# Half-height weight loads and wider zero products at the start of a fused attention and feed-forward kernel

## The chip, the cores and the metric

The kernel runs on one core of a Trainium2 chip. A core has a matrix engine (TensorE, PE in the profile; its weight loads stand apart as PEld), three engines for everything else (VectorE or DVE, ScalarE or ACT, GpSimd or POOL), a sequencer that issues most transfers (SyncE, SP), and 16 DMA engines that carry them. The metric is the device time of one execution in microseconds (us), the median of several runs.

## The reference

Eight batches with eight heads of attention over 576 positions, 64 channels each, then a two-layer feed-forward network over all 4608 tokens:

```python
scores = scale * np.matmul(q, k.transpose(0, 1, 3, 2))
rel = pos[:, None] - pos[None, :]
mask_local = (rel >= 0) & (rel < stride)              # heads 0 to 3, stride 32
mask_strided = (rel >= 0) & (pos[None, :] % stride == pos[:, None] % stride)   # heads 4 to 7
attn = softmax(where(mask, scores, -1e9)); attn_out = attn @ v
x = attn_out as 4608 x 512
h = x @ w_in                                          # 512 x 2048
g = where(h >= 1, h, where(h <= -1, 0, (h + 1) ** 2 / 4))
out = g @ w_out                                       # 2048 x 512
```

All inputs are 32-bit floats, but the feed-forward weights come as 64-bit ones and reach the kernel as pairs of 32-bit words.

## The kernel before, in words

The feed-forward work is cut along the 2048 inner columns into 16 units f of 128, and along the tokens into chunks of 512. A unit has two parts i: part 0 holds its columns of w_in, part 1 its rows of w_out, each as 128 partitions of 512 pairs of words, 4096 bytes a partition, 512 KB. `load_w(f, i)` (lines 312 to 320) brings one part into a tile named raw with one transfer on SP's queue. Its optional argument `after` first copies one element of a loaded q/k tile into the raw tile (line 318, on ACT), which holds the transfer, and all that stands behind it on SP, until that q/k tile has landed.

A raw part is then converted by steps named by letters: A (line 343, ACT) and L (line 347, ACT) scale the high and the low words, B (line 351, DVE) shifts, C (line 355, POOL) adds, D (line 364, ACT, or DVE under the name G) rounds to the matrix engine's 32-bit format, E (line 368, DVE) takes what the rounding left. "A10" is step A of unit 1, part 0. Every step reads all 128 partitions of its part. The products use high and low halves, three products for one.

The first three chunks of tokens are done unit by unit: `up` (line 775) makes h for a unit from x, ACT and DVE apply g, `down` (line 820) adds into four accumulators. Later chunks use weights combined beforehand (lines 388 to 408) in seven products in place of eight, lines 917 and 1005.

Attention runs batch by batch, in four units of rows u. Its steps are named by letters too: s scores (line 482), o and i open and close their accumulators with products of zeros and of the mask (lines 497 and 506), g copies out (line 538), x, a or b, e, q, p or k, r or w the softmax (lines 568 to 596), f flips by the matrix engine (line 609), c or d keeps the result (line 619), v multiplies by v (line 669), h and l write x as high and low parts (lines 730 and 739). From batch 1 on the probabilities are turned through DRAM: line 643 writes them, and line 654 gathers them with four transfers of 32 partitions each, to partitions 0, 32, 64 and 96 in this order.

The order of the work is written out by hand, and each engine does its instructions in that order. `BEGIN` (lines 29 to 34) is the order of the start, the attention of batch 0 with the conversions of units 0 to 2. In it "Zs0:17" is 17 products of zeros into the accumulators of score unit 0 (`zero`, lines 460 to 467), "Zv0" and "Zf0" the same into those of v and of the flips; the real work overwrites what they write. Later lists (`WORK`, `CONV`, `SUMS` and so on) hold times by which the rest is sorted once, when the program is built.

The loads of the start are issued on SP in this order (lines 1044 to 1059): q/k of batch 0 in four transfers; part 0 of unit 0, held by line 318; two transfers of v; part 0 of unit 1; two of v; part 0 of unit 2; then, in `stage`, part 1 of units 0, 1 and 2, both parts of unit 3; two q/k transfers of batch 1; both parts of units 4 and 5; then v of batch 1, and further units as their places come free.

Of the kernel before, what the change touches and what calls it, by code (L numbers as in the profile page):

```python
# [17 lines left out]
P = 128  # L18
# [8 lines left out]
GATE, ROUNDED = (0.31, 2.01), (1.62, 3.18)  # L27

BEGIN = """
Zs0:17 o0 s0 o1 i0 X0 s1 i1 S0 o3 g1 x1 s2 Zv0:3 Zf0:3 m2 e0 a1 A00 s3 i3 e1 x2 q0 p0 g3 a2 q1 Zf0:9  # L30
e2 w0 Zf0:5 f0 p1 x3 c0 B00 v0 b3 L00 e3 r1 q2 p2 f1 C00 r2 q3 A10 d1 D00 p3 h0 r3 L10 l0 A20 v1 B10
f2 h1 d2 f3 c3 v3 l1 H1 L20 C10 G10 v2 E10 M0 M1 h3 B20 l3 E00 h2 H3 C20 U0 l2 G20 V0 M3 U1 H2 M2
E20 V1
"""
# [139 lines left out]
def tile_sparse_attention_then_ffn(  # L174
# [14 lines left out]
    nc = tc.nc  # L189
# [28 lines left out]
    def slots(u):  # L218

        n, rest = divmod(UNITS[u][2], IL if UNITS[u][0] else IS)  # L220
        return n + (rest > 0), n
# [50 lines left out]
    for i in range(IL):  # L272
        part = slice(i * QL, (i + 1) * QL)
        for n0, n1, off in ((0, SLOTS, ST),) if i else ((0, 1, 0), (1, SLOTS, ST)):
            t = m_loc[part, n0:n1]
# [4 lines left out]
    for i in range(IS):  # L280
        t = m_str[i * QS:(i + 1) * QS]
# [20 lines left out]
    wt, raws, pieces, held = {}, {}, {}, set()  # L302
    PLACES = (6, 7, 8, 9, 10, 11, 12, 13, 14, 15, 12, 13, 14, 15)
    w_v = w.bitcast(U32).rearrange("f p (i e t) -> f p i e t", i=2, t=2)
# [4 lines left out]
    def place(u, shape, dtype, name):  # L309
        return slot(f"w{u}", shape, dtype, name)  # L310

    def load_w(f, i, after=None):
        at = PLACES[f]
        if i == 0:
            held.add(at)
            raws[f] = place(at, [P, 2, DM, 2], U32, f"raw_{f}")
        if after is not None:
            nc.scalar.copy(raws[f][0:1, i, 0:1, 0].bitcast(F32), after)
        nc.sync.dma_start(raws[f][:, i], w_v[f][:, i])
        pieces[f, i] = [(raws[f][:, i], slice(0, DM))]  # L320

    def load_piece(f, i, k=0, pool=qk_p, tag="qk", of=1):
# [51 lines left out]
    def stage(n=len(PLACES)):  # L374
        nonlocal staged
        while staged < n and ((staged, 0) in pieces or PLACES[staged] not in held):
            if (staged, 0) not in pieces:
                load_w(staged, 0)
            load_w(staged, 1)
            staged += 1  # L380
# [65 lines left out]
    def attention(b, kinds):  # L446
# [3 lines left out]
        def banks(u, kind):  # L450

            if (u, kind) in ahead:
                return ahead.pop((u, kind))
            local, _, nb = UNITS[u]
            Q, W = (QL, WL) if local else (QS, WS)
            shapes = {"s": [[P, slots(u)[0], 2, W]] * 2, "f": [[P, n, P] for n in slots(u)], "v": [[P, nb, Q]] * 2}[kind]
            name = {"s": "sc", "f": "tp", "v": "xp"}[kind]
            return [psum(kinds(u, kind, j), shape, f"{name}_{b}_{u}_{j}") for j, shape in enumerate(shapes)]

        def zero(u, kind, n):  # L460

            ahead[u, kind] = ts = banks(u, kind)
            names = [f"a{k}" for k in range(len(ts[0].shape) - 1)]
            t = ts[0].rearrange(f"p {' '.join(names)} -> p ({' '.join(names)})")
            N = min(t.shape[1], 256)
            for _ in range(n):
                nc.tensor.matmul(t[:, :N], zeros, zeros[:, :1].broadcast_to([P, N]), start=True, stop=True)

# [39 lines left out]
        def homes(u):  # L508
# [3 lines left out]
            ns = slots(u)  # L512
            N = 2 * sum(ns)
            size = [P, 2 * SLOTS * 2, 64]
            if b == 0 and u >= 2:
                room = place(NF - 1 - u, size, F32, f"pr_{b}_{u}")
            else:
                room = s_p.tile(size, F32, tag="s", name=f"pr_{b}_{u}")
            st = st_p.tile([P, 3, 2 * SLOTS * 2], F32, tag="st", bufs=4, name=f"st_{b}_{u}")[:, :, :N]
            pr = room[:, :N, :W]  # L520
            if W < 64:
                nc.gpsimd.memset(room[:, :N, W:], 0.0)
            todo = [(j, slice(0, P), 0, ns[1], j * ns[0]) for j in range(2)]
# [226 lines left out]
        def go(names):  # L750
            for name in names.split():
                if name[0] == "Z":
                    zero(int(name[2]), name[1], int(name[4:]))
                    continue
                steps[name[0]](int(name[1]))
# [287 lines left out]
    with tc.manual_schedule():  # L1043
        for p in range(4):
            load_qk(0, p)
        load_w(0, 0, loaded[0, 1, "qk"][0:1, 0, 0:1])
        load_v(0, 0)
        load_v(0, 1)
# [44 lines left out]
        for c in range(CLASSIC):  # L1093
            for f in range(NF):
                t = 4 * (NF * (c - 1) + f)
# [17 lines left out]
        for s in range(NSC):  # L1113
            t = 4 * NF * (CLASSIC - 1) + 2 * len(UP) * s
# [61 lines left out]
```

## Time and profile before

| | |
|---|---|
| median of 3 runs | 818.4 us (817.62 to 819.12) |
| span of the profiled execution, first to last instruction | 815.5 us, 2.9 less than the median |
| granted TensorE clock, mean | 1.000 |
| busy share of the span | PE 99%, PEld 81%, DVE 70%, ACT 61%, POOL 29% |
| HBM read and written | 147.26 MB and 46.66 MB, 238 GB/s over the span |
| first product of line 775 | starts at 24.06 us |

The profile is that of one execution. A row of a group gives the line, the engine, the operation, the tiles (out<-in, buffer numbers left out), shapes and count, busy time and mean duration, and the idle time of the engine before it with what ended it. A row of the timeline gives start, length, engine, line, and in square brackets the idle time before it with its releaser. SPq is SP's queue: its rows are issues of transfers, and the length is that of the issue, not of the transfer. A row on issues ends with the KB of one and the median time from issue to landing.

### The profile page before, as it was taken

What the parts mean: (1) busy time and instruction counts of PE and PEld (TensorE: products, weight loads), DVE (VectorE), ACT (ScalarE), POOL (GpSimd) and SP (SyncE); (2) the same over time, 40 slices, a digit from 0 to 9 for tenths busy, and PEclk for the clock granted to TensorE, in tenths of its full rate; (3) what the DMA queues carried; (4) which work ended last, traced back from release to release, by engine and by line L of the source; (5) the groups of instructions that cost most, each with busy time, mean ns of one, the idle gap of its engine ahead of it and who ended that gap; (6) DMA issues with size and microseconds to landing.
All of it is one profiled execution on the core that took longest, in us unless ns stands there. A gap on an engine that the chain in (4) does not pass through costs nothing.

```text
span 815.5 us, 17861 instructions
## 1 busy us (share of the span) xinstructions
PE 806.2 (99%) x6969; PEld 656.9 (81%) x6969; DVE 574.7 (70%) x850; ACT 495.4 (61%) x866; POOL 232.5 (29%) x226
## 2 busy tenths in 40 slices
PE   8999999999999999999999999999999999999998
PEld 6788888878878888887878888888888888888886
DVE  5898868767548477776778876675589834558664
ACT  5888955545355365776775453778654647775442
POOL 5353544873347543023222000220120001114100
PEclk9999999999999999999999999999999999999999
DMA  9936437788868867987998768887666776666765
GB/s 344 408 138 201 153 111 274 265 298 278 265 221 299 286 243 257 304 287 247 285 288 266 216 203 249 263 265 228 193 193 213 232 235 196 196 192 190 216 200 170
DMA packets 101796, 195.10 MB, mean 239 GB/s; under 512 B 17105, under 2 KB 32465, under 8 KB 99665
## 3 DMA queue, kind: packets, MB, share of 16 engines
q1 hardware_dynamic: 92496, 164.60, 63.3%
q10 hardware_dynamic: 9216, 29.36, 9.4%
q8 instruction: 55, 0.90, 0.5%
q14 instruction: 29, 0.23, 0.1%
HBM read 147.26 MB, written 46.66 MB: 238 GB/s over the span
## 4 chain that ended last, share of the span: by engine, by line
PE 91%; DMA 5%; issue 1%; DVE 1%; ACT 1%; POOL 0%; SPq 0%; ACTq 0%; POOLq 0%
PE o L820 16%; PE h L775 16%; PE yo L1005 15%; PE y L917 15%; PE zo L1005 8%; PE z L917 7%; PE xo L1005 4%; PE x L917 4%; PE xp L669 3%; PE sc L482 3%; DMA wr<-kq 1%; DMA qk<-in_qk_s 1%; DMA there<-t 1%; DMA pT<-there 1%; DMA qk<-in_qk_l 1%
## 5 line engine op out<-in xcount | busy, mean ns | idle before, releaser
L917 PE MATMUL y<-x,wr 128*128 128x512 f32 x576 | 141.3, 392 | 0.0
L775 PE MATMUL h<-xq,w 128*128 128x512 f32 x576 | 140.0, 392 | 0.1
L1005 PE MATMUL yo<-hl,wr 128*128 128x512 f32 x576 | 132.8, 390 | 0.6 <-DMA wr<-kq 0.6
L820 PE MATMUL o<-gh,w 128*128 128x512 f32 x384 | 130.1, 399 | 0.0
L1005 PEld LDWEIGHTS yo<-hl,wr 128*128 128x128 f32 x576 | 108.0, 188 | 23.4 <-DMA wr<-kq 1.0
L775 PEld LDWEIGHTS h<-xq,w 128*128 128x128 f32 x576 | 107.4, 188 | 23.4 <-DVE xq L739 0.7
L917 PEld LDWEIGHTS y<-x,wr 128*128 128x128 f32 x576 | 107.4, 188 | 22.7
L820 PEld LDWEIGHTS o<-gh,w 128*128 128x128 f32 x384 | 72.1, 188 | 16.2
L820 PE MATMUL o<-gl,w 128*128 128x512 f32 x192 | 75.0, 391 | 0.0
L917 PE MATMUL z<-x,wr 128*128 128x512 f32 x288 | 73.7, 391 | 0.0
L957 POOL TENSOR_TENSOR ga<-gb,ga 128x1024 f32<-128x1024 f32 x9 | 21.6, 2397 | 167.5 <-DVE ga L785 141.7
L1005 PE MATMUL zo<-hl,wr 128*128 128x512 f32 x288 | 66.1, 390 | 0.0
L572 POOL TENSOR_TENSOR pr<-pr,st 128x384 f32<-128x384 f32 (+3 forms) x21 | 26.3, 1253 | 135.7 <-DVE st L595 64.5
L1005 PEld LDWEIGHTS zo<-hl,wr 128*128 128x128 f32 x288 | 54.0, 188 | 11.3
L917 PEld LDWEIGHTS z<-x,wr 128*128 128x128 f32 x288 | 53.8, 188 | 11.3
L782 ACT ACTIVATE tmp<-tmp 128x512 f32<-128x512 f32 x96 | 60.7, 632 | 3.0
L871 DVE TENSOR_TENSOR hl<-ga,hl 128x1024 fp32r<-128x1024 f32 x36 | 47.3, 1315 | 19.9 <-ACT hl L870 18.2
L870 ACT CAST hl<-ga 128x1024 fp32r<-128x1024 f32 x36 | 38.0, 1056 | 35.1 <-PE yo L1005 12.6
L396 POOL TENSOR_TENSOR xs<-w 128x512 f32<-128x512 f32 x32 | 45.1, 1426 | 48.4 <-DMA ks<-xs 32.8
L785 DVE SCALAR_TENSOR_TENSOR h<-h,u 128x512 f32<-128x512 f32 x47 | 32.8, 697 | 30.5 <-ACT u L782 30.1
L398 POOL TENSOR_TENSOR xs<-xs 128x256 f32<-128x256 f32 x64 | 51.3, 802 | 5.0
L779 ACT ACTIVATE u<-h,half 128x512 f32<-128x512 f32 x48 | 33.1, 689 | 29.6 <-PE h L775 24.1
(120 smaller groups left out, 1321.9 us busy)
## 6 DMA issues: line engine op xcount, KB each, us to landing
wr<-ks SPq DMA_DIRECT2D x192, 256.0 KB, 3.9
wr<-kq SPq DMA_DIRECT2D x144, 256.0 KB, 3.4
ks<-xs ACTq DMA_DIRECT2D x16, 1024.0 KB, 4.8
raw<-in_w SPq DMA_DIRECT2D x30, 512.0 KB, 9.6
kq<-w ACTq DMA_DIRECT2D x48, 256.0 KB, 3.8
qk<-in_qk_s SPq DMA_DIRECT2D x16, 604.0 KB, 6.1
qk<-in_qk_l SPq DMA_DIRECT2D x16, 576.0 KB, 6.0
v<-in_v_l SPq DMA_DIRECT2D x21, 384.0 KB, 6.0
```

The source lines that it names most:

```text
L396: nc.gpsimd.tensor_tensor(out=b[:, :, f] if i else b[:, f], in0=hi, in1=lo, op=ALU.add)
L398: nc.gpsimd.tensor_tensor(out=st[:, to, HF:], in0=st[:, x, HF:], in1=st[:, y, HF:], op=op)
L572: eng.tensor_tensor(out=pr, in0=pr, in1=st[:, 0].unsqueeze(2).broadcast_to(list(pr.shape)), op=ALU.add)
L775: nc.tensor.matmul(o_ps[c, f], wt[f][:, 0, h, x, e:e + P], xq[c][:, y, cc], start=first and n == 0, stop=last and n == len(todo) - 1)
L779: nc.scalar.activation(u, h, AF.Relu, bias=half, scale=0.5)
L782: nc.scalar.activation(u, u, AF.Square)
L785: nc.vector.scalar_tensor_tensor(out=to, in0=h, scalar=1.0, in1=u, op0=ALU.max, op1=ALU.min)
L820: nc.tensor.matmul(o_ps[c][d], wt[f][:, 1, h, x, e:e + P], gs[y], start=f == 0 and n == 0, stop=f == NF - 1 and n == 2)
L870: nc.scalar.copy(t[:, 0], src)
L871: nc.vector.tensor_tensor(out=t[:, 1], in0=src, in1=t[:, 0].bitcast(F32), op=ALU.subtract)
L917: nc.tensor.matmul(to, w_[:, a, c * P:(c + 1) * P], xc[m][:, b, c], start=m in (1, 2, 5) and c + q == 0, stop=c == 1 and q == 2, skip_grou ...
L1005: nc.tensor.matmul(to, w_[jj][:, a, d * P:(d + 1) * P], t[:, b, jj], start=m in (1, 2, 5) and k + jj + q == 0, stop=k == NP // 2 - 1 and j ...
```

## The change

Loads of units 0 to 5 become two transfers each, of partitions 0 to 63 and 64 to 127. The products of zeros get up to 384 columns in place of 256 (every accumulator concerned has 384), and their counts in `BEGIN` go from 17, 3, 3, 9 and 5 to 11, 2, 2, 6 and 3.

```diff
 BEGIN = """
-Zs0:17 o0 s0 o1 i0 X0 s1 i1 S0 o3 g1 x1 s2 Zv0:3 Zf0:3 m2 e0 a1 A00 s3 i3 e1 x2 q0 p0 g3 a2 q1 Zf0:9
-e2 w0 Zf0:5 f0 p1 x3 c0 B00 v0 b3 L00 e3 r1 q2 p2 f1 C00 r2 q3 A10 d1 D00 p3 h0 r3 L10 l0 A20 v1 B10
+Zs0:11 o0 s0 o1 i0 X0 s1 i1 S0 o3 g1 x1 s2 Zv0:2 Zf0:2 m2 e0 a1 A00 s3 i3 e1 x2 q0 p0 g3 a2 q1 Zf0:6
+e2 w0 Zf0:3 f0 p1 x3 c0 B00 v0 b3 L00 e3 r1 q2 p2 f1 C00 r2 q3 A10 d1 D00 p3 h0 r3 L10 l0 A20 v1 B10
...
-        nc.sync.dma_start(raws[f][:, i], w_v[f][:, i])
+        n = P // 2 if f < 6 else P
+        for p in range(0, P, n):
+            nc.sync.dma_start(raws[f][p:p + n, i], w_v[f][p:p + n, i])
         pieces[f, i] = [(raws[f][:, i], slice(0, DM))]
...
-            N = min(t.shape[1], 256)
+            N = min(t.shape[1], 384)
             for _ in range(n):
                 nc.tensor.matmul(t[:, :N], zeros, zeros[:, :1].broadcast_to([P, N]), start=True, stop=True)
```

## The prediction

> **What bounds the kernel now.** I read the page's head first, then the busy time by stretches, then the chain of waits over the first 31 us.
>
> ```profile
> span 815.5 us, 17861 instructions
> PE 806.2 (99%) x6969; PEld 656.9 (81%) x6969; DVE 574.7 (70%) x850; ACT 495.4 (61%) x866; POOL 232.5 (29%) x226
> ```
>
> ```profile
> 5.00:10.00 5.00, 4.31 (x201) 3.28 (x202) 2.31 (x5) 1.39 (x6) 1.69 (x7) 1.00 0.99 377
> 10.00:15.00 5.00, 4.24 (x67) 3.26 (x68) 4.93 (x10) 3.59 (x10) 2.22 (x3) 1.00 0.98 372
> ...
> 20.00:24.00 4.00, 2.91 (x97) 2.29 (x94) 3.44 (x11) 3.13 (x12) 1.63 (x3) 1.00 1.03 414
> 24.00:30.00 6.00, 5.92 (x35) 4.36 (x24) 4.89 (x17) 4.67 (x16) 1.68 (x2) 1.00 1.02 408
> ...
> 100.00:800.00 700.00, 698.77 (x5661) 571.42 (x5660) 487.03 (x677) 410.34 (x693) 183.77 (x158) 1.00 0.75 240
> ```
>
> The columns are stretch, length, then busy us of TensorE (PE), its weight loads, VectorE (DVE), ScalarE (ACT) and GpSimd (POOL), then granted clock, busy share of the DMA engines, and GB/s. From 100 to 800 us TensorE is busy 698.77 of 700: nothing the diff touches is there, and whatever the change does to the start is carried to the end, microsecond for microsecond. In the first 24 us TensorE has gaps, and two things are full: the DMA engines (shares 0.98 to 1.03) and the chain of conversions and softmax steps.
>
> ```profile
> 11.95 1.27 POOL pr L572
> 13.22 2.83 issue
> ...
> 16.91 1.01 POOL raw L355
> ...
> 17.94 0.66 ACT w L364
> ...
> 19.93 0.70 ACT raw L343
> ...
> 21.37 0.96 PE xp L669 x32
> ...
> 27.08 3.26 PE h L775 x13
> 30.34 0.67 PE sc L482 x46
> ```
>
> So from about 12 us the end is set by POOL and ACT working down their queues (the gap called "issue" has no releaser in the profile), until the dense products of line 775 take over. Among the chain's steps are the conversions of raw weights (L343 is step A, L355 step C, L364 step D), which the changed loads feed. What the loads cost now:
>
> ```profile
> ACT raw L343 <- DMA raw<-in_w: 0.9, 1, 0.9
> ```
>
> ```profile
> 11.42 0.68 ACT L343 ACTIVATE raw<-raw 128x512 f32<-128x512 f32 x1 [0.93 <-DMA raw<-in_w]
> ...
> 16.97 0.71 ACT L343 ACTIVATE raw<-raw 128x512 f32<-128x512 f32 x1
> ...
> 17.94 0.66 ACT L364 CAST w<-raw 128x512 fp32r<-128x512 f32 x1 [0.26 <-POOL raw L355]
> ```
>
> Between 10 and 24 us ACT waits for a load once, 0.93 us, for the first weights. The second step A starts at 16.97 unhindered, the third at 19.93 (in the chain above). How close behind the data they run comes from the issues and their times to landing (last number):
>
> ```profile
> 6.61 0.33 SPq L319 DMA_DIRECT2D raw<-in_w  x1
> 6.98 0.43 SPq L431 DMA_DIRECT2D v<-in_v_l  x1
> 7.45 0.43 SPq L431 DMA_DIRECT2D v_None<-in_v_l  x1
> 7.93 0.69 SPq L319 DMA_DIRECT2D raw<-in_w  x1
> ```
>
> ```profile
> 10.25 0.64 SPq L319 DMA_DIRECT2D raw<-in_w  x1
> ```
>
> ```profile
> 18.61 0.33 SPq L418 DMA_DIRECT2D qk<-in_qk_l  x1
> ```
>
> ```profile
> raw<-in_w SPq DMA_DIRECT2D x1, 512.0 KB, 4.8
> ```
>
> ```profile
> raw<-in_w SPq DMA_DIRECT2D x1, 512.0 KB, 8.8
> ```
>
> ```profile
> raw<-in_w SPq DMA_DIRECT2D x1, 512.0 KB, 9.6
> ```
>
> ```profile
> qk<-in_qk_l SPq DMA_DIRECT2D x1, 576.0 KB, 10.5
> ```
>
> In that order: unit 0 lands at 6.61 + 4.8 = 11.4 (used 11.42), unit 1 at 16.7 (used 16.97), unit 2 at 19.85 (used 19.93), and the second q/k pair of batch 1 at 29.1. TensorE reaches that pair in the second half of these 96 products, at about 30.8:
>
> ```profile
> 30.27 1.17 PE L482 MATMUL sc<-qk 64*32 64x64 f32 x96
> ```
>
> So the conversions run 0.0, 0.2 and 0.1 us behind their data, and the pair has 1.7 us of slack. That is what decides.
>
> **The change, part by part.** *The split.* Units 0 to 5 have two loads each, so 12 transfers of 512 KB become 24 of 256 KB. Nothing is computed on half a tile: the first reader needs both halves. The bytes, the queue and their order stay, so the second half lands when the whole did, provided the transfers run as fast. Three costs.
>
> SP issues 12 times more. The issues above cost 0.33 to 0.69 us of SP; each row's data waits behind 2 to 9 us of earlier data (times to landing 4.8 to 10.5), so the queue hides an extra issue. Only for unit 0 is the lead short: its second half is issued some 0.4 us after the first, while the first occupies the DMA engines 0.26 MB / 408 GB/s = 0.64 us. Hidden, with 0.2 us to spare; without cover it costs 0.2 to 0.4 us. The first load waits for a landed q/k transfer (through the one-element copy of L318); the loads of v, unit 1 and unit 2 are queued behind it on SP, and come later by 0.4 us an extra issue, which against their lead is nothing.
>
> SP also waits for older transfers:
>
> ```profile
> SPq L319 <- DMA raw<-in_w: 9.5, 9, 2.1
> ```
>
> Nine of its loads waited for an earlier landing; so the transfers in flight are limited in number, and 256 KB ones put fewer bytes in flight. From 408 GB/s and some 10 us to landing, 4 MB are in flight, about eight loads. Eight of half the size are 8 x 0.64 = 5.1 us of data, still above the shortest time to landing shown, 4.8. I take 0 and keep 1 us for it. A second semaphore for each reader has no row; I take 0.1 us in all.
>
> The rate of a transfer that covers 64 partitions has no row either. The nearest is the gather of line 654, four transfers of 32 partitions each, the first two on partitions 0 to 63:
>
> ```profile
> 519.26 1.81 SPq L654 DMA_DIRECT2D pT<-there  x4
> ```
>
> ```profile
> DMA packets 182, 0.14 MB, mean 320 GB/s; under 512 B 24, under 2 KB 164, under 8 KB 182
> ...
> q1 hardware_dynamic: 182, 0.14, 95.2%
> ```
>
> The second is the stretch from 521.55 to 522.0 us, while the gather's packets (between 512 B and 2 KB) are 164 - 24 = 140 of 182. The engines are 95.2% busy and move 320 GB/s, with packets under half of the weights' 4 KB (512 KB over 128 partitions). That is far above half of the 408 GB/s that the weights get. So one end is no loss (1.28 us a load, as now); the other is that each half gets half the rate, 1.28 us more a load. I take no loss, by the gather, which is the nearest row; it is short (0.45 us), so the other end stays in the range.
>
> The Trainium skill speaks against the change here: its page "SBUF — State Buffer", section "Door 1: The DMA port swizzle", says that a transfer on partitions 0 to 63 reaches only 8 of 16 ports and was measured at 196 GB/s against 328 for 128 partitions, and the section "Can I just issue two DMAs to hit both halves?" that two such transfers serialize. By its ratio each load would take 0.67 x 1.28 = 0.86 us more, an estimate that, put through the steps of rival A, gives 823.6 us. The gather's stretch does not agree with it, but does not settle it for longer rows.
>
> *The products of zeros.* 37 of 256 columns (9472) become 24 of 384 (9216).
>
> ```profile
> 0.98 3.58 PE L467 MATMUL sc<-zeros 128*128 128x256 bf16 x17 [0.98 <-DVE zeros L264]
> ...
> 5.00 0.72 PE L482 MATMUL sc<-qk 64*32 64x64 f32 x48
> ```
>
> ```profile
> 12.11 1.72 PE L467 MATMUL tp<-zeros 128*128 128x256 bf16 x14
> ```
>
> ```profile
> 14.46 0.73 PE L609 MATMUL tp<-ident,pr 128*128 128x128 f32 x5 [0.63 <-DVE pr L596]
> ```
>
> The first group: 3.58 / 17 = 0.211 us each, 0.316 at 384 columns, 11 of them 3.48 us, so 0.1 us less. The next work of weight starts at 5.00, when q and k land; the gain is hidden by that. The third and fourth groups run together: 1.72 us for 14 becomes 1.72 x 9 x 384 / (14 x 256) = 1.66, and TensorE waits 0.63 us for DVE after it anyway. The second groups keep their columns (768 each). Price 0; if the cover were gone, 0.1 us of gain.
>
> The sum: 0 for issues, 0 for the rate, 0.1 for second waits, 0 for zeros: 815.5 becomes 815.6. The median of the three runs shown, 818.4, is 2.9 above the profiled span; I take that as constant: 818.5.
>
> **The rivals.** *A, each half at half rate.* Every load is 1.28 us longer. Unit 0 lands at 12.7: ACT is 1.3 late. Unit 1 lands at 16.7 + 2.6 = 19.3, ACT arrives at 18.3 and waits 1.0; the cast behind it already waited 0.26 for POOL, so ACT is 2.0 late. Unit 2 lands at 19.85 + 3.85 = 23.7, ACT arrives at 21.9, 3.8 late. TensorE's dense work is as late. The second q/k pair has eight longer loads ahead of it (units 0, 1, 2, then 0 to 2's other halves and both of 3): 29.1 + 10.3 = 39.4, and TensorE arrives at 30.8 + 3.8 = 34.6: 4.8 more. In all 8.6: 827.1. For it: the same DMA engines write half as many partitions. Against: the gather. It decides once a load is over 0.1 us longer, for unit 0's lateness passes to ACT undiminished.
>
> *B, the halves partly overlap*, because the 16 DMA engines are not in step: 0.64 us more a load. By the same steps: unit 0 0.64; unit 1 lands at 18.0, ACT there at 17.6, 0.8 in all; unit 2 at 21.8 against 20.7, 1.9 in all; the pair at 34.2 against 32.7, 3.4 in all: 821.9.
>
> *C, the first load lands sooner*, since the DMA engines begin it after a smaller issue. At most the 0.93 us wait goes: 818.5 - 0.9 = 817.6. For it: rates of 377 and 372 GB/s before 15 us against 414 after. Against: unit 0's bytes still end with the second half. A gain beyond it would need POOL's unexplained 2.83 us to shorten, and nothing in the diff says so.
>
> *D, the columns lost let the clock drop*, by 0.1 us of idle time at 4.4 us. The granted clock is 1.00 in every stretch, and TensorE already waits 0.5 us there. Price: the 3 us of work from 5 to 8 us at half speed would be 3 us, half of it hidden by waits: 820.
>
> **How the numbers follow.** Forecast 0.50, A 0.14, B 0.20, C 0.13, D 0.03. The time is the forecast's, 818.5, whose own range is 817.4 to 819.6 (no gain but the 0.93 us, and 1 us for bytes in flight). The range of 8 in 10 goes from 816.9, C with 0.7 us for run-to-run spread (the runs lie from 817.62 to 819.12), to 824.0, which holds B and the estimate from the page; it leaves out A and C's far end. A measurement of this kernel tells about 0.2%, 1.6 us, from no change: faster beyond it only C's far end, 0.09; slower A, B and D, 0.36, with a little of the forecast's upper end not counted; within 0.55.
>
> **What would show it.** Right: step A for unit 0 starts at 11.3 to 11.6, the third step A by 20.1, the DMA rate from 20 to 24 us stays over 400 GB/s, TensorE's products of line 775 settle into dense work at about 27.1, and the chain has no new DMA row. Rate wrong: GB/s in 10 to 30 us falls towards 200 to 270, ACT shows waits of 1 us and more for raw weights, and TensorE waits for q/k near 33 us. Flight limit wrong: the DMA share falls under 0.9 while SP waits for landings. Zeros wrong: a granted clock below 1.00 before 24 us, or a wait after the fill groups that is not DVE's or DMA's. The forecast fails if any load is late by more than ACT's own queue.

## The result, and the profile after

The changed kernel takes 828.11 us (825.23 to 831.01, 6 runs) against 817.66 before (815.91 to 819.12, 6 runs): a ratio of 1.013, with an interval of 1.0109 to 1.0151. It is slower by 1.3%, and outside the range forecast. The profiled execution has a span of 825.7 us, 10.2 more than before. Line numbers after line 319 are two higher.

The same views as before, first the page's head and the busy time by stretches (stretch, length, busy us of PE, PEld, DVE, ACT, POOL, granted clock, busy share of the DMA engines, GB/s):

```profile
span 825.7 us, 17870 instructions
PE 812.5 (98%) x6956; PEld 660.5 (80%) x6956; DVE 574.6 (70%) x850; ACT 496.4 (60%) x866; POOL 231.9 (28%) x226
```

```profile
10.00:15.00 5.00, 4.04 (x79) 2.53 (x79) 3.52 (x8) 2.33 (x8) 2.22 (x3) 1.00 1.02 290
15.00:20.00 5.00, 3.85 (x102) 3.55 (x102) 3.96 (x8) 4.29 (x11) 2.47 (x3) 0.70 1.03 257
20.00:24.00 4.00, 3.70 (x62) 3.17 (x60) 2.35 (x7) 2.12 (x6) 2.54 (x3) 0.50 1.04 243
24.00:30.00 6.00, 5.86 (x105) 5.02 (x104) 5.04 (x15) 4.29 (x18) 1.22 (x2) 0.73 1.04 247
...
35.00:40.00 5.00, 1.45 (x85) 1.24 (x88) 4.61 (x8) 4.97 (x9) 2.03 (x2) 0.75 1.04 260
...
100.00:800.00 700.00, 698.80 (x5707) 570.77 (x5707) 484.26 (x678) 414.28 (x705) 186.25 (x161) 1.00 0.74 236
```

From 100 to 800 us nothing has changed. From 20 to 30 us the DMA engines move 243 to 247 GB/s where they moved 408 to 414, and their busy share is as high as ever. The clock, 1.00 throughout before, falls to half in two stretches: it is 0.50 from 17 to 24 us and again from 38 to 44.

Who waits for the late data, from the groups of waits of ACT (8 to 48 us) and TensorE (0 to 60), and step A of units 0, 1 and 2 from ACT's timeline:

```profile
ACT raw L345 <- DMA raw<-in_w: 6.2, 4, 2.6
```

```profile
PE sc L484 <- DMA qk<-in_qk_l: 4.3, 2, 2.7
```

```profile
12.98 0.67 ACT L345 ACTIVATE raw<-raw 128x512 f32<-128x512 f32 x1 [2.63 <-DMA raw<-in_w]
...
18.77 0.69 ACT L345 ACTIVATE raw<-raw 128x512 f32<-128x512 f32 x1 [0.24 <-DMA raw<-in_w]
...
23.46 0.69 ACT L345 ACTIVATE raw<-raw 128x512 f32<-128x512 f32 x1 [1.87 <-DMA raw<-in_w]
```

The chain that ended last, over the first 48 us:

```profile
6.92 5.96 DMA raw<-in_w
...
12.98 0.67 ACT raw L345
...
27.70 11.75 DMA qk<-in_qk_l
39.45 0.04 issue
39.49 0.97 PE sc L484 x48
40.46 4.73 PE h L777 x12
```

Before, the chain from 12 us on had no transfer in it; now it runs through the first weights and then through the second q/k pair of batch 1, which TensorE takes up at 39.49 instead of about 30.8, 8.7 later. The twelve products after it take 4.73 us, because the clock is at half for most of that time (0.50 from 38 to 44 us). In an experiment below with the clock up, the same twelve take 2.94. That is 1.8 more: 8.7 + 1.8 = 10.5, against 10.2 between the two profiled spans.

### The profile page after: what moved, and what is told of

It reads as the page before. It is cut to its first block, busy times and chain, and to the rows that moved or that the text cites. A ratio compares the mean times of both kernels' runs of the same rounds, so it can differ in the third digit from the quotient of the medians.

```text
span 825.7 us, 17870 instructions
## 1 busy us (share of the span) xinstructions
PE 812.5 (98%) x6956; PEld 660.5 (80%) x6956; DVE 574.6 (70%) x850; ACT 496.4 (60%) x866; POOL 231.9 (28%) x226
## 4 chain that ended last, share of the span: by engine, by line
PE 94%; DMA 4%; ACT 0%; DVE 0%; SPq 0%; issue 0%; ACTq 0%
PE o L822 17%; PE yo L1007 16%; PE h L777 16%; PE y L919 15%; PE zo L1007 8%; PE z L919 7%; PE xp L671 4%; PE xo L1007 4%; PE x L919 4%; PE sc L484 3%; DMA qk<-in_qk_l 2%; DMA wr<-kq 1%; DMA raw<-in_w 1%; DMA wr<-ks 1%; PE tp L611 1%
## 5 line engine op out<-in xcount | busy, mean ns | idle before, releaser
L777 PEld LDWEIGHTS h<-xq,w 128*128 128x128 f32 x576 | 108.8, 190 | 23.7 <-DVE xq L741 0.7
L822 PEld LDWEIGHTS o<-gh,w 128*128 128x128 f32 x384 | 72.1, 188 | 16.4
L873 DVE TENSOR_TENSOR hl<-ga,hl 128x1024 fp32r<-128x1024 f32 x36 | 47.3, 1314 | 19.5 <-ACT hl L872 19.3
```

What stands on the lines that cost most here:

```text
L777: nc.tensor.matmul(o_ps[c, f], wt[f][:, 0, h, x, e:e + P], xq[c][:, y, cc], start=first and n == 0, stop=last and n == len(todo) - 1)
L822: nc.tensor.matmul(o_ps[c][d], wt[f][:, 1, h, x, e:e + P], gs[y], start=f == 0 and n == 0, stop=f == NF - 1 and n == 2)
L873: nc.vector.tensor_tensor(out=t[:, 1], in0=src, in1=t[:, 0].bitcast(F32), op=ALU.subtract)
```

## The experiments

Three theories were set against each other. P: a transfer to 64 partitions of one half runs slower. N: smaller transfers put too few bytes in flight. Z: the products of zeros let the clock lapse.

**The two parts alone, and the cut along the other dimension.** e1 has the split of the loads only, e2 the products of zeros only. e3 cuts each load along the columns in place of the partitions:

```diff
-        nc.sync.dma_start(raws[f][:, i], w_v[f][:, i])
+        n = DM // 2 if f < 6 else DM
+        for e in range(0, DM, n):
+            nc.sync.dma_start(raws[f][:, i, e:e + n], w_v[f][:, i, e:e + n])
```

Expected of e1:

> The loads split as in the change, the products of zeros as before. If the split alone makes the time (theory P: a transfer on half of the partitions runs at a lower rate, 240 to 260 GB/s from 20 to 30 us in place of 408), the ratio to before is 1.010 to 1.015, as for the change. If the products of zeros have a part in it (theory Z: fewer columns, so a later or a lapsing clock), the ratio is clearly under 1.010 and the granted clock stays 1.00 before 24 us.

Expected of e2:

> The products of zeros as in the change (384 columns, 24 of them), the loads whole. Theory P: ratio 1.000, within 0.002, first product of line 775 (here 24 to 24.2 us) as before, clock 1.00 throughout. Theory Z: slower by 2 to 5 us with stretches at clock 0.5 before 30 us.

Expected of e3:

> The same loads cut in two along the columns: 24 transfers of 256 KB, each on all 128 partitions with 2 KB rows; zeros as before. Theory P: DMA rate from 20 to 30 us back to 390 to 410 GB/s, ratio 1.000 to 1.002. Theory N (the number of transfers in flight is limited, so transfers of half the size halve the bytes in flight and with them the rate): 240 to 260 GB/s and a ratio near 1.012, as for the split by partitions.

The ratios were 1.0124 (1.0099 to 1.0149) for e1, 0.9995 (0.9974 to 1.0017) for e2 and 0.9997 (0.9971 to 1.0023) for e3. The stretch from 20 to 30 us of the changed kernel, then of e1, e2 and e3:

```profile
20.00:30.00 10.00, 9.55 (x165) 8.19 (x163) 7.39 (x21) 6.42 (x23) 3.76 (x4) 0.64 1.04 245
```

```profile
20.00:30.00 10.00, 6.96 (x135) 5.66 (x128) 7.32 (x20) 6.06 (x22) 3.22 (x4) 0.79 1.04 240
```

```profile
20.00:30.00 10.00, 9.29 (x131) 7.02 (x135) 8.88 (x28) 8.48 (x26) 3.60 (x4) 1.00 1.03 410
```

```profile
20.00:30.00 10.00, 8.64 (x121) 6.68 (x119) 8.10 (x26) 7.52 (x25) 3.01 (x4) 1.00 1.00 350
```

The split alone makes the whole loss, the zeros none (Z falls), and as many transfers of the same size on all 128 partitions cost nothing measurable (N falls as the cause). e3's 350 is under the 390 to 410 expected, and no run here shows why, but nothing that sets the end was late by it: its chain enters the dense products of line 777 at 27.28 us, where the kernel before entered them at 27.08.

**Which loads count.** e4 splits units 4 and 5 only, e5 part 0 of units 0 to 2, e6 the five loads behind these:

```diff
-        n = P // 2 if f < 6 else P
+        n = P // 2 if f in (4, 5) else P              # e4
+        n = P // 2 if i == 0 and f < 3 else P         # e5
+        n = P // 2 if f == 3 or i == 1 and f < 3 else P   # e6
```

Expected of e4:

> Only units 4 and 5 are split by partitions (8 transfers of 256 KB for 4 of 512 KB), zeros as before. If what counts is the lateness of unit 0 to 2 on ACT and of the q/k pair of batch 1 on TensorE, which all stand ahead of these loads, nothing is late: the rate falls to about 250 GB/s only from about 29 to 38 us and the ratio is 0.998 to 1.002. If the slower rate costs wherever it is, the 4 loads cost a third of the change, 1.004.

Expected of e5:

> Split by partitions only for part 0 of units 0, 1 and 2, the loads that step A on ACT follows at once; zeros as before. With 0.84 us more a load (1.06 us for each 256 KB half in the changed kernel's profile against 1.28 for the whole before), ACT is late by 0.8 after unit 0, 1.2 after unit 1 and 2.5 after unit 2, and the q/k pair is no longer waited for (29.1 + 2.5 = 31.6 against 33.3): ratio 1.003 if the steps of rival A hold with this size. If the lateness on ACT is absorbed by its queue, 1.000.

Expected of e6:

> Split only for part 1 of units 0 to 2 and both parts of unit 3: the five loads between the first three and the q/k pair of batch 1. Zeros as before. ACT is not late; the pair lands 5 x 0.84 = 4.2 us later, at 33.3, and TensorE, there at 30.8, waits 2.5: ratio 1.003, with TensorE's wait for q/k of that size in the profile. If that wait is absorbed later (TensorE has something else to do, or the pair is not needed), 1.000.

e4 came out at 1.0003 (0.9985 to 1.0021). Its rate from 29 to 37 us is as low as the changed kernel's, with TensorE busy all the time:

```profile
29.00:37.00 8.00, 8.00 (x126) 6.46 (x125) 6.35 (x12) 7.94 (x15) 3.08 (x3) 1.00 1.02 238
```

So a slow load costs only where somebody stands behind it. e5 came out at 1.0056 (1.0038 to 1.0073), e6 at 1.0049 (1.0032 to 1.0067): each about 4 to 4.6 us where 2.5 was expected. The loads before step A and those before the pair both cost, and both were sized too small. In e5, step A of the three units:

```profile
13.61 0.66 ACT L345 ACTIVATE raw<-raw 128x512 f32<-128x512 f32 x1 [3.72 <-DMA raw<-in_w]
20.35 0.67 ACT L345 ACTIVATE raw<-raw 128x512 f32<-128x512 f32 x1 [1.16 <-DMA raw<-in_w]
25.69 0.67 ACT L345 ACTIVATE raw<-raw 128x512 f32<-128x512 f32 x1 [2.69 <-DMA raw<-in_w]
```

Unit 0 is already 13.61 - 11.42 = 2.2 us late, not 0.8, and unit 2 is 25.69 - 19.93 = 5.8 us late, not 2.5. The rate from 15 to 20 us shows part of why, although whole transfers of v are among what moves then:

```profile
15.00:20.00 5.00, 3.13 (x93) 2.81 (x96) 4.54 (x10) 3.70 (x11) 1.83 (x3) 0.84 1.04 254
```

So the whole transfers queued among the slow ones were not at their old rate either. In e6 the pair lands at 25.37 + 9.59 = 34.96 us (chain), 4.2 after 30.8, which is about the whole loss of 4.0:

```profile
25.37 9.59 DMA qk<-in_qk_l
34.96 0.04 issue
35.00 0.72 PE sc L484 x45
35.73 2.94 PE h L777 x12
```

But TensorE waits for the pair only 0.40 us there, not 2.5, because it comes late itself:

```profile
21.15 0.67 ACT L345 ACTIVATE raw<-raw 128x512 f32<-128x512 f32 x1 [1.14 <-DMA raw<-in_w]
```

```profile
26.92 6.86 PE L777 MATMUL h<-xq,w 128*128 128x512 f32 x24
33.71 0.89 PE L484 MATMUL sc<-qk 64*32 64x64 f32 x48
35.00 0.72 PE L484 MATMUL sc<-qk 64*32 64x64 f32 x48 [0.40 <-DMA qk<-in_qk_l]
```

Part 0 of unit 2 is loaded whole in e6 and stands ahead of the split loads, and still step A waits 1.14 us for it and starts at 21.15, 1.2 late; in e4, where the split loads are further behind, it starts at 19.65. "ACT is not late" was wrong, then: split loads slow a whole one in front of them. The dense products start at 26.92, 2.9 after 24.06, and run in part at a lower clock (0.72 from 24 to 30 us). The pair alone would set the same end, but e6 doesn't show it alone.

e5 and e6 together, 4.6 + 4.0 us, are most of the change's 10.5, though the two aren't cleanly apart.

**The clock.** e7 is the changed kernel with more products of zeros where TensorE stands:

```diff
-e2 w0 Zf0:3 f0 p1 x3 c0 B00 v0 b3 L00 e3 r1 q2 p2 f1 C00 r2 q3 A10 d1 D00 p3 h0 r3 L10 l0 A20 v1 B10
+e2 w0 Zf0:14 f0 p1 x3 c0 B00 v0 b3 L00 e3 r1 q2 p2 f1 C00 r2 q3 A10 d1 D00 p3 h0 r3 L10 l0 A20 v1 B10
...
-WORK = {1: [(-60.38, 's0'), ...
+WORK = {1: [(-60.38, 'Zs0:26 s0'), ...
```

> The change with more products of zeros: 14 for 3 before the first flip, and 26 ahead of the scores of batch 1, where TensorE stands and waits, so that the clock doesn't fall to half. If the stretches at clock 0.5 cost part of the time (theory Z2: 2 to 4 us of the 10), the ratio falls to 1.007 to 1.010 with clock 1.00 to 50 us; if only the late data cost, it stays at 1.012 to 1.014.

The ratio was 1.0132 (1.0098 to 1.0166). The clock was below 1.00 only from 24 to 30 us (0.72), not in the two long stretches of the changed kernel, and the twelve products behind the pair ran at full speed; but the pair landed 0.6 us later:

```profile
28.28 11.73 DMA qk<-in_qk_l
40.01 0.04 issue
40.05 0.72 PE sc L484 x45
40.78 2.94 PE h L777 x12
```

The clock's 1.8 us is seen in the profile; whether it is seen in the time these runs can't tell, since the interval is wider than that. The half clock follows from the waits: e1 and e5 have the products of zeros as before, and their clock falls too (0.64 from 24 to 30 us in e1, 0.50 from 20 to 24 in e5). In e1 it holds at 1.00 up to 24 us, where the changed kernel has 0.50 from 17 on, and the two take the same time within their intervals. So the stretch from 17 to 24 us cost nothing that was measured; TensorE waits for the pair behind it in any case.

**Place or number.** e8 cuts each load into partitions 0 to 31, 32 to 95 and 96 to 127, e9 into four of 32:

```diff
+        cuts = (0, 32, 96, 128) if f < 6 else (0, 128)        # e8
+        for p, p1 in zip(cuts, cuts[1:]):
+            nc.sync.dma_start(raws[f][p:p1, i], w_v[f][p:p1, i])
```

Expected of e8:

> Units 0 to 5 in three transfers each, of partitions 0 to 31, 32 to 95 and 96 to 127; zeros as before. If the partitions' place counts, as the port table of the Trainium skill has it (32 to 95 reaches all ports, the outer two half of them), a load takes 128 KB at 247 GB/s twice and 256 KB at 408 once, 1.7 us, so 290 to 320 GB/s from 20 to 30 us. If the number of partitions of a transfer counts, whatever their place, at most 247 GB/s.

Expected of e9:

> Units 0 to 5 in four transfers each of 32 partitions, zeros as before. If the rate goes by the half of the partitions that a transfer lies in (partitions 0 to 31 reach as many ports as 0 to 63, by the port table of the Trainium skill), 230 to 260 GB/s from 20 to 30 us, as for halves; if it goes by the number of partitions, half of that, 120 to 140 GB/s.

One run each. From 17 to 24 us, e8 and then e9:

```profile
17.00:24.00 7.00, 4.83 (x162) 3.99 (x158) 5.40 (x15) 5.54 (x17) 5.04 (x5) 1.00 1.03 280
```

```profile
17.00:24.00 7.00, 4.74 (x156) 3.93 (x156) 4.78 (x13) 4.35 (x11) 5.20 (x5) 1.00 1.04 245
```

Quarters move as much as halves, so it isn't the number of partitions. e8, at 280, is short of the 290 to 320 expected and over the 247 of the other theory: a miss, and too near to both to decide. From 24 to 30 us the DMA engines of both were idle for part of the time (share 0.72 in e8, 0.64 in e9), which neither e1 (1.03) nor e3 (0.99) showed, while SP waited for earlier loads to land (2.8 us in 7 waits from 18 to 30 us in e9). That fits a limit on transfers in flight that binds with three or four small transfers a load. Both took longer than before all the same: 825.6 us for e8 and 827.3 for e9.

So e11 and e12 show the rate by itself, with half of these weights left out: e11 loads only partitions 0 to 63 of units 0 to 5, e12 only 32 to 95.

```diff
+        if f < 6:
+            for p, p1 in ((64, 128),):                    # e12: ((0, 32), (96, 128))
+                nc.gpsimd.memset(raws[f][p:p1, i].bitcast(F32), 0.0)
+            nc.sync.dma_start(raws[f][0:64, i], w_v[f][0:64, i])     # e12: 32:96
```

Expected of e11:

> The disputed cost by itself: of units 0 to 5 only partitions 0 to 63 are loaded, one transfer of 256 KB for each load, and the upper 64 partitions of each raw tile are set to zero by POOL, so half of these weights is left out. If a transfer on 64 partitions of one half is slow by itself, the loads land about 1.06 us apart or more (at most 250 GB/s); if only the alternation of halves was slow, 0.64 us apart (400 GB/s). The time itself is not compared, since POOL has 12 fills more.

Expected of e12:

> The same with partitions 32 to 95 loaded and the outer 64 set to zero: as many partitions, bytes and transfers as in the run beside it, half of them from each half of the partitions. If the place decides (the port table of the Trainium skill), 0.64 to 0.70 us a load, 375 to 410 GB/s; if the number of partitions or the 4 rows for each DMA engine decide, the same rate as with partitions 0 to 63.

A stretch in which these loads move, e11 from 19.5 to 25 us, then e12 from 15.5 to 19.5:

```profile
DMA packets 344, 1.17 MB, mean 212 GB/s; under 512 B 66, under 2 KB 66, under 8 KB 343
...
q1 hardware_dynamic: 343, 1.15, 102.0%
```

```profile
DMA packets 475, 1.65 MB, mean 412 GB/s; under 512 B 84, under 2 KB 84, under 8 KB 474
...
q1 hardware_dynamic: 474, 1.63, 101.5%
```

As many partitions and bytes, the same queue, packets of the same size, and 212 against 412 GB/s: the place decides. The last whole transfer of v lands at 22.0 us in e11 and at 16.4 in e12; after that, from 22 to 25 and from 16.5 to 20 us, the rates are 215 and 412. ACT and DVE stand idle in e12's stretch, but that doesn't make its rate: they stand idle in most of e10's below too, where halves move 245. This is what the Trainium skill says on its page "SBUF — State Buffer", section "Door 1: The DMA port swizzle": partitions 0 to 63 share 8 of 16 ports, and bit 6 of the partition's number picks the other 8; 32 to 95 has both. Its limit for 8 ports, about 218 GB/s, agrees with the 212 here.

**Both halves at once.** e10 issues the upper halves on ACT's queue:

```diff
+            (nc.scalar if p else nc.sync).dma_start(raws[f][p:p + n, i], w_v[f][p:p + n, i])
```

> The split of the change, but the upper half of each load is issued by ACT on its own queue, so that both halves are in flight together; zeros as before. If the limit is at the partitions' side and the DMA engines take turns between the two queues, the rate from 20 to 30 us is back over 350 GB/s; if the halves follow each other all the same, 240 to 270 GB/s. The time itself is not to be compared, since ACT issues 12 transfers more in the midst of its conversions.

From 17 to 30 us (q10 is ACT's queue):

```profile
DMA packets 1059, 3.19 MB, mean 245 GB/s; under 512 B 183, under 2 KB 183, under 8 KB 1059
...
q1 hardware_dynamic: 592, 1.67, 54.0%
q10 hardware_dynamic: 467, 1.52, 49.9%
```

Each queue had about half of the engines' time, and the rate is what it was on one queue. It doesn't help, as the same page of the Trainium skill says in "Can I just issue two DMAs to hit both halves?". The page measured 6% over a single transfer; here 245 is some 15% over the 212 of one half alone. Whole transfers of v are among SP's bytes until about 29 us; from 30 to 35 us the rate is 238. Whether at each moment a lower half on one queue stood against an upper half on the other can't be read here.

## Why the prediction was wrong

- **The step that failed** is the term for the rate in the sum, "0 for the rate": "I take no loss, by the gather, which is the nearest row". A pair of halves takes 2 x 256 KB at 245 GB/s, 2.14 us, against 1.28: 0.86 more a load, on twelve loads, of which the first eight have somebody behind them. The signs that the prediction set for a wrong rate all came: the GB/s (from 15 us on), ACT's waits for raw weights, TensorE's wait for q/k.
- **The reading of the gather** was wrong too. The 320 GB/s of its 0.45 us were not all its own. Each of its four transfers, and the weights that were loaded beside it, have this size:

```profile
pT<-there SPq DMA_DIRECT2D x3, 96.0 KB, 3.8
```

```profile
wr<-ks SPq DMA_DIRECT2D x1, 256.0 KB, 4.4
```

  The first is 3 KB a partition in four pieces, 768 B each; the second goes to 128 partitions, 2 KB each. So the 140 middling packets are 0.108 MB, 239 GB/s, and the other 18 large ones 0.037 MB, 82 GB/s, of whole loads. 239 is what halves in alternation move here; read so, the gather gave no ground for "no loss". In the next half microsecond (522.0 to 522.5 us) it is nearly alone and the rate is 276; which of its lower and upper transfers move at which moment can't be read, so that stays open. I also read the busy share of 95.2% as if it spoke for the rate; in the changed kernel it is 1.04 at 245 GB/s from 20 to 30 us, in e2 1.03 at 410.
- **The estimate from the page "SBUF — State Buffer" of the Trainium skill**, 0.86 a load, met the measured 0.86, and was given less weight than the gather. The agreement is partly luck: one half alone has 212 GB/s here against 412 for partitions 32 to 95, a factor of 1.9 where the page's 196 and 328 give 1.7, and halves in alternation do better than one half alone. And with 0.86 put through rival A's steps the time is 823.6, inside the range and 4.5 us short of 828.1. So the rate alone isn't all: the pair lands at 39.45 where these steps put it at 29.1 + 8 x 0.86 = 36.0, 3.5 later, because whole loads beside the split ones were slow as well (e5, e6), and the clock adds 1.8.
- **Rival A** had the course right and was given 0.14. It put unit 0 at 12.7 (used at 12.98), unit 1 at 19.3 (18.77), unit 2 at 23.7 (23.46), the pair at 39.4 (taken up at 39.49) and the end at 827.1 (828.1). Partly by luck: half the rate, 1.28 more a load, is too much for these transfers (0.86), but whole loads beside the split ones were slow as well, which A left out (unit 0 was already 1.6 us late, not 0.86), and the clock's 1.8 us is missing from it.
- **Rival B** had the rate nearly right (0.64 more a load, measured 0.86) and the end too early, 821.9, for these two reasons besides.
- **The issues and the bytes in flight** cost nothing, as taken: e3 makes the 12 extra issues with no loss, and its readers wait for two transfers a load as well, so no run shows the 0.1 us that was put down for second waits. The 1 us kept for the flight limit wasn't needed with two pieces a load; with three and four the DMA engines ran empty for a time.
- **The products of zeros** cost nothing, as taken (e2). Rival D was wrong in its cause: the clock fell in the changed kernel, but after TensorE had stood waiting, first 1.86 us up to 15.91, for work behind the late weights of unit 0; with whole loads and the same zeros it is 1.00 over the first 100 us (e2).
- **What is carried to the end**: right. Nothing was won back between 100 and 800 us.
- **The range**, up to 824.0, left out A. The rows against A were one stretch of 0.45 us with other traffic in it; on such ground the far end, each half at half the rate, belonged in the range.

## What to carry to other kernels

Cut a load along the columns, so that each piece keeps all 128 partitions (e3, no loss), and not into upper and lower halves. A single piece of 64 partitions that straddles partition 64 ran at the full 412 GB/s (e12), but it leaves the outer partitions over: the cut into three with such a middle piece still took 825.6 us in its one run (e8). Read the rate of a stretch of transfers from its GB/s, not from the engines' busy share, and count by size whose packets they are. Before pricing a slower load, look who stands behind it: splitting the first three loads cost 0.6% and the next five 0.5%, and the last four, just as slow, nothing.

## What the runs showed that was not expected

- Slow transfers slow the whole ones beside them in the queue. In e5 only three loads are split, and the rate from 15 to 20 us, with whole transfers of v under way, is 254 GB/s; step A of unit 2 is 5.8 us late where three times 0.86 were to be expected. In e6 a whole load ahead of the split ones lands 1.2 us late. How it comes about was not measured.
- Halves in alternation move 238 to 247 GB/s, one half alone 212. The alternation wins back some of the loss, not most of it; why was not measured.
- Half the clock came with waits, as in 20 to 24 us (0.50) of the changed kernel, although TensorE is shown busy 3.70 of 4 us there.
